# The attention products with the values stationary, in four column parts of the tensor engine

## The chip, the cores and the metric

The kernel runs on one core of one Trainium2 chip. The metric is the device time of one execution, in microseconds (us). A core has five engines that run side by side and meet through semaphores: TensorE (PE, matrix products into the PSUM banks), VectorE (DVE), ScalarE (ACT, activation functions), GpSimd (POOL) and SyncE (SP, which issues all DMAs of this kernel). Every engine works through its own instructions strictly in the order in which they were written.

## The reference, cut to what matters

Inputs are q, k and v of shape 8 x 8 x 576 x 64 (batch, head, position, channel) and the parameters of a feed-forward part.

```python
scores = q @ k.T / sqrt(64);  mask: block i sees blocks j <= i, blocks of 64
attn   = exp(scores - max);   attn = attn / sum(attn)
x      = concat over heads of attn @ v             # 8 x 576 x 512
x_prev = x shifted by one position inside a batch
xk = mu_k * x + (1 - mu_k) * x_prev                # the "mix"
xr = mu_r * x + (1 - mu_r) * x_prev
k  = relu(xk @ w_k);  v = (k * k) @ w_v            # 512 -> 1024 -> 512
out = sigmoid(xr @ w_r) * v
```

The kernel leaves out the subtraction of the maximum. It forms the sigmoid from a tanh, with the factor one half folded into `w_v`.

## The kernel before, in words

The positions of all batches, 8 x 576 = 4,608, form one row. Attention works by batch (`b`), the feed-forward part by chunks (`c`) of 512 positions, nine of them; a chunk crosses the border between two batches.

For each batch q and k are loaded, cast to bf16 and turned so that the channel lies on partitions (for the first two batches by PE products, `add_long_qkt`; for the others by a DMA transpose, `add_qk`). `add_scores` multiplies k by q, two heads side by side in the two halves of PE's rows (L675). ACT takes the exponential (L697), which gives unnormalized probabilities with key positions on partitions; POOL sets the masked corners to zero (L705). An `e` buffer holds the probabilities of one pair of heads; there are three.

`add_av` (L717) then takes each head's 128 x 128 pieces of the probabilities as the stationary operand and streams the values, 64 columns and a column of ones, past them: 15 products per head (L738). The result has the query position on partitions, the 65th column is the sum. DVE takes the reciprocal of the sums (L758, five per partition) and multiplies (L759) into the tile `x`. `add_xt` (L802) turns `x` on PE in fp32 (L812), four 128 x 128 pieces to one PSUM bank, and ACT copies the turned pieces into `xt` (L791), which has channels on partitions and positions along the row.

`add_mix` (L840) forms the difference to the previous position (`d`, L851, on POOL or DVE) and from it xk and xr (L863, DVE). `add_pk` multiplies by `w_k` (L899), ACT applies the relu (L909) and DVE squares (L915). `add_pr` multiplies by `w_r` (L928), ACT takes the tanh (L938). `add_pv` multiplies the squares by `w_v` (L957), DVE multiplies by tanh plus one (L967), and SP stores the result (L973).

The order of the instructions is fixed when the program is built. Every step is a task with an engine, an estimated duration, a rank, the tasks that it depends on and the buffers that it takes. `Plan.order` runs through time with these estimates: an engine that is free takes the task of lowest rank whose dependencies and buffers are ready by the estimates. `RANK` holds the ranks, the order of the loads, and for `flex` tasks the engine. The rings give the number of buffers: PSUM has two banks for scores (`s`, each two banks wide), two for attention results (`m`) and two for the feed-forward part (`mm`); batch 0's attention results use `mm`. On the chip an instruction that isn't ready holds everything behind it on its engine. `fill` tasks (L996) are products of an identity matrix with no use for the result; they come last in rank and so stand where the plan has nothing else for PE.

Of the kernel before, what the change touches and what calls it, by code (L numbers as in the profile page):

```python
# [24 lines left out]
RANK = {  # L25
 'loads': ['g0q', 'g0k', 'v4', 'b1g0q', 'g1q', 'v2', 'wk4', 'wv3', 'g1k',
           'wk6', 'b1g1k', 'v0', 'v3', 'v1', 'wk1', 'b1g0k', 'wk3', 'b1v0',
           'wk0', 'mu', 'wr1', 'b1g1q', 'wk5', 'b1v2', 'wk2', 'wv7', 'wv2',
           'wk7', 'wv6', 'wv0', 'b1v3', 'wv5', 'wv1', 'wv4', 'b1v1',
           'b1v4', 'wr0', 'wr3', 'wr2'],  # L30
 'cast k': 73.0,
 'cast r': -238.0,
 'cast v': 217.5,
 'qkt0': [1111.0, 118.5],
 'score0': [-518.5, -654.0, -419.5, -913.5, -522.5, -642.5, -671.0, -497.0,
            -421.0, -801.5, -464.0, -766.0, -967.5],
 'av0': [-570.0, -764.5, -682.5, -522.0, -807.5, -750.0, -447.5, -733.0],
 'xt0': [-283.0, -183.5, -390.5, -555.0, -237.5],
 'mix0': [-428.0, -99.5, 191.5, 92.0],
 'pk0': [-241.5, -17.5, -339.0, -413.0, -149.5, -278.5, -81.5, -167.0],  # L40
 'pr0': [60.5, 55.5, -497.5, -275.5],
 'pv0': [62.0, -164.0, -8.0, 48.0],
 'qk': [33.5, 38.0, 37.0, 41.0],
 'v': 46.0,
 'qkt': [418.0, -487.5],
 'turn': -17.0,
 'av': -416.0,
 'xt': 6.5,
 'mix': 646.5,
 'xr': 4.0,  # L50
 'moe': 63.0,
 'eng': {'v32': 'POOL',
         'wk7': 'ACT',
         'qk201': 'DVE',
         'long0010': 'DVE',
         'v71': 'POOL',
         'd61': 'POOL',
         'd42': 'POOL',
         'qk701': 'DVE',
         'v70': 'ACT',  # L60
         'd02': 'POOL',
         'd41': 'DVE',
         'v64': 'DVE',
         'qk511': 'DVE',
         'v72': 'DVE',
         'long0000': 'DVE',
         'wv0': 'POOL',
         'd33': 'POOL',
         'qk611': 'DVE',
         'qk300': 'POOL',  # L70
         'd51': 'POOL',
         'v23': 'POOL',
         'long0110': 'DVE',
         'qk501': 'POOL',
         'd10': 'POOL',
         'ev0010': 'DVE',
         'v03': 'POOL',
         'd01': 'POOL',
         'long1110': 'DVE',
         'qk700': 'ACT',  # L80
         'v20': 'POOL',
         'v01': 'DVE',
         'qk601': 'POOL',
         'qk321': 'POOL',
         'v14': 'POOL',
         'qk620': 'POOL',
         'v51': 'ACT',
         'd20': 'DVE',
         'v41': 'POOL',
         'qk331': 'POOL',  # L90
         'qk430': 'POOL',
         'd32': 'POOL',
         'qk520': 'POOL',
         'long0001': 'ACT',
         'd53': 'POOL',
         'd81': 'POOL',
         'v73': 'DVE',
         'v40': 'ACT',
         'd31': 'POOL',
         'qk221': 'ACT',  # L100
         'd43': 'DVE',
         'qk420': 'ACT',
         'qk211': 'POOL',
         'v43': 'POOL',
         'qk730': 'POOL',
         'v21': 'POOL',
         'v54': 'DVE',
         'qk720': 'POOL',
         'wk6': 'POOL',
         'qk320': 'POOL',  # L110
         'd72': 'POOL',
         'v62': 'POOL',
         'd62': 'POOL',
         'qk500': 'POOL',
         'qk401': 'POOL',
         'v31': 'DVE',
         'd52': 'POOL',
         'long1111': 'POOL',
         'wv6': 'POOL',
         'v63': 'POOL',  # L120
         'wk0': 'ACT',
         'qk411': 'DVE',
         'qk510': 'DVE',
         'long0011': 'ACT',
         'v50': 'ACT',
         'd22': 'POOL',
         'v00': 'ACT',
         'qk210': 'ACT',
         'v61': 'DVE',
         'd82': 'POOL',  # L130
         'ev0000': 'ACT',
         'qk630': 'POOL',
         'v53': 'POOL',
         'v60': 'POOL',
         'v10': 'POOL',
         'wr2': 'POOL',
         'd23': 'DVE',
         'qk721': 'POOL',
         'qk421': 'POOL',
         'd11': 'POOL',  # L140
         'long1000': 'DVE',
         'qk310': 'POOL',
         'qk710': 'POOL',
         'long0111': 'POOL',
         'ev0101': 'DVE',
         'qk311': 'ACT',
         'wk2': 'DVE',
         'd71': 'POOL',
         'v52': 'POOL',
         'qk530': 'ACT',  # L150
         'qk220': 'ACT',
         'v04': 'POOL',
         'd73': 'DVE',
         'qk610': 'DVE',
         'd80': 'POOL',
         'long1100': 'POOL',
         'd60': 'POOL',
         'qk631': 'POOL',
         'qk600': 'POOL',
         'd83': 'POOL',  # L160
         'qk400': 'ACT',
         'v74': 'POOL',
         'v44': 'DVE',
         'v42': 'DVE',
         'long0100': 'DVE',
         'qk531': 'ACT',
         'long0101': 'DVE',
         'd70': 'POOL',
         'd40': 'POOL',
         'qk301': 'POOL',  # L170
         'qk330': 'POOL',
         'd63': 'POOL',
         'qk231': 'POOL',
         'qk230': 'POOL',
         'v30': 'POOL',
         'd30': 'POOL',
         'qk711': 'DVE',
         'ev0001': 'ACT',
         'd50': 'DVE',
         'qk521': 'POOL',  # L180
         'long1101': 'DVE',
         'wk3': 'DVE',
         'qk431': 'POOL',
         'd00': 'POOL',
         'qk621': 'ACT',
         'qk731': 'ACT',
         'd03': 'POOL',
         'wk5': 'POOL',
         'qk410': 'DVE',
         'v02': 'POOL',  # L190
         'ev0011': 'DVE',
         'v34': 'POOL',
         'qk200': 'POOL',
         'long1001': 'POOL',
         'ev1011': 'ACT',
         'v22': 'POOL',
         'wv5': 'POOL',
         'wk4': 'POOL',
         'wv4': 'DVE',
         'v11': 'POOL',  # L200
         'wr1': 'POOL',
         'v13': 'ACT',
         'long1010': 'POOL',
         'long1011': 'POOL',
         'v33': 'POOL',
         'wk1': 'DVE',
         'wv1': 'ACT',
         'wv7': 'POOL',
         'd12': 'DVE',
         'ev1000': 'ACT',  # L210
         'wv2': 'DVE',
         'd13': 'POOL',
         'ev0111': 'ACT',
         'ev1010': 'ACT',
         'v12': 'POOL',
         'ev1101': 'DVE',
         'ev1111': 'ACT',
         'wv3': 'ACT',
         'd21': 'DVE',
         'ev0100': 'DVE',  # L220
         'ev1110': 'DVE',
         'wr0': 'ACT',
         'ev1001': 'ACT',
         'ev0110': 'DVE',
         'v24': 'ACT'},
}


class Plan:
# [4 lines left out]
    LATENCY = {"PE": 0.12, "ACT": 0.08, "DVE": 0.08, "POOL": 0.1, "SP": 2.4}  # L234
# [85 lines left out]
def kernel(  # L320
# [21 lines left out]
    D1 = D + 1  # L342
# [6 lines left out]
    RINGS = {"ld": 10, "vl": 5, "nl": 4, "nb": 4, "tl": 2, "qkt": 2, "e": 3,  # L349
             "x": 4, "r": 4, "xt": 2, "d": 3, "xk": 2, "xr": 2, "kr": 3,  # L350
# [17 lines left out]
    identf = consts.tile([P, P], FP)  # L368
    make_identity(nc, identf)
    VOs = [consts.tile([P, 5, H, D1 + 1], F16, name=f"VO{i}") for i in range(2)]  # L370
    E4s = [consts.tile([P, H, P], F16, name=f"EL{i}") for i in range(2)]
# [11 lines left out]
    for i in range(2):  # L383
        nc.vector.memset(VOs[i][:, :, :, D:D1], 1.0)
        nc.vector.memset(VOs[i][D:P, 4], 0.0)
        nc.vector.memset(E4s[i], 0.0)
    for nb in NBs:
        nc.gpsimd.memset(nb[D:P, :, 4], 0.0)
# [23 lines left out]
    def flex(key, alts, rank, fn, deps, takes=(), uses=()):  # L412


        eng = RANK["eng"].get(key, next(iter(alts)))
        t = plan.add(eng, alts[eng], rank, lambda: fn(eng), deps, takes, uses)
        t["key"], t["alts"] = key, alts
        return t
# [22 lines left out]
    def add_qk(b, pr, rank, turn_rank):  # L441
        nb = plan.buf("nb")
        for n, src in enumerate((q, k)):
# [10 lines left out]
            def fn(eng, n=n, key=key):  # L454
# [7 lines left out]
                f"qk{b}{pr}{n}", {"POOL": 0.76, "DVE": 0.7, "ACT": 0.65}, rank, fn,  # L462
# [46 lines left out]
    CAST = {"POOL": 0.72, "DVE": 0.77, "ACT": 0.7}  # L509
# [36 lines left out]
    def add_v(b, ranks):  # L546
        for sc in range(5):
# [8 lines left out]
            def fn(eng, n=n, sc=sc):  # L556
                convert(eng, VOs[b % 2][0:n, sc, :, 0:D],
                        tiles["vl", b, sc][0:n])
            cast["v", b, sc] = flex(
                f"v{b}{sc}", {"POOL": 0.73, "DVE": 0.7, "ACT": 0.65},  # L560
# [4 lines left out]
    def add_w(name, n, ranks, rank):  # L565
        src = {"k": moe_w_k, "r": moe_w_r, "v": moe_w_v}[name]
        src = src.rearrange("(cc p) (n j) -> n cc p j", p=P, j=C)
        for i in range(n):
            ld = plan.buf("ld")
            cc, half = (i % CCn, i // CCn) if name == "k" else (i, 0)  # L570
            t = load(("w", name, i), lambda: new("ld", [P, S], FP),
                     lambda d, cc=cc, half=half: [(d[:, 0:C], src[half, cc])],
                     ranks[i], 0.8, takes=[ld])


# [525 lines left out]
```

The softmax here doesn't subtract the row's maximum and nothing guards it: scores larger than these inputs give would overflow.

## Time and profile before

| What | Value |
|---|---|
| Three runs | 274.95, 276.27, 277.6 us (median 276.27) |
| Profiled execution, span | 274.9 us (the page gives no other time for it) |
| PE, products | 262.7 us busy, 96% (2,676 instructions) |
| PE, weight loads | 151.8 us, 55% |
| DVE | 209.1 us, 76% |
| ACT | 196.6 us, 72% |
| POOL | 129.3 us, 47% |
| DMA, share of the engines | 82% over the span; near one until about 210 us, low afterwards |
| Value products (L738) | 960, 193 ns each from start to end |
| Turning products (L812) | 160, 273 ns each from start to end |
| Copies into `xt` (L791) | 68, 23.1 us |
| Normalization (L758, L759) | 64 of each, 188 and 492 ns |

The span runs from the first instruction to the last. Products are pipelined: the duration of one, from its start to its end, is much longer than the distance to the next, so counts times durations say little for PE, and a busy PE is not one at its peak. For the other engines the distance is close to the duration. The granted PE clock was 0.998 of full speed.

### The profile page before, as it was taken

How to read it: one execution, taken by the hardware profiler on the slowest of the kernel's cores; microseconds unless marked ns; L12 is line 12 of the kernel's file. 1: busy time of each engine (PE TensorE's matmuls, PEld its weight loads, DVE VectorE, ACT ScalarE, POOL GpSimd, SP SyncE). 2: the span in 40 equal slices, each digit the busy share in tenths (PEclk: the TensorE clock that was granted, in tenths of full speed). 3: DMA queues.
4: the chain of work that ended last, by engine and by line, in shares of the span. 5: the costliest groups of instructions: out<-in, count | busy, mean ns of one | idle time of the engine just before them, and what ended most of it. 6: DMA issues, size and time to landing. Idle time of an engine off the chain costs nothing.

```text
span 274.9 us, 7043 instructions
## 1 busy us (share of the span) xinstructions
PE 262.7 (96%) x2676; PEld 151.8 (55%) x2676; DVE 209.1 (76%) x373; ACT 196.6 (72%) x315; POOL 129.3 (47%) x275
## 2 busy tenths in 40 slices
PE   8989997999999999999999999989999999999995
PEld 8777774555465546555654465446554655444443
DVE  4647796789789767897988687938898876996642
ACT  2689886876898688887888888776867883460630
POOL 3156898364457465573661353733845152601000
PEclk9999999999999999999999999999999999999999
DMA  7989999789999999999989988999999002102113
GB/s 221 346 237 263 308 325 213 170 191 203 239 189 214 214 207 245 206 207 214 232 169 235 206 222 196 220 205 259 193 195 257 4 0 79 76 0 88 66 41 114
DMA packets 137617, 51.32 MB, mean 187 GB/s; under 512 B 128240, under 2 KB 128496, under 8 KB 137584
## 3 DMA queue, kind: packets, MB, share of 16 engines
q1 hardware_dynamic: 137584, 50.88, 82.4%
q8 instruction: 21, 0.34, 0.5%
q14 instruction: 12, 0.10, 0.1%
HBM read 33.56 MB, written 9.44 MB: 156 GB/s over the span
## 4 chain that ended last, share of the span: by engine, by line
PE 65%; DMA 11%; DVE 9%; POOL 7%; issue 3%; SPq 3%; ACT 1%; POOLq 0%; DVEq 0%; ACTq 0%
PE t_mm L899 18%; PE t_mm L957 18%; PE t_mm L928 8%; PE t_m L738 8%; PE t_s L675 6%; PE t_m L812 4%; DMA t_ld<-in_k_dram 4%; SPq L406 2%; DVE t_xk L863 2%; DMA t_ld<-in_q_dram 2%; POOL WV L431 2%; DVE t_xr L863 2%; DMA t_vl<-in_v_dram 2%; DMA t_ld<-in_moe_w_k_dram 2%; DVE t_x L759 1%
## 5 line engine op out<-in xcount | busy, mean ns | idle before, releaser
L697 ACT ACTIVATE t_e<-t_s 128x1024 f16<-128x1024 f32 x96 | 96.3, 1027 | 15.8 <-PE t_s L675 15.5
L899 PE MATMUL t_mm<-t_xk,WK 128*128 128x512 f16 x288 | 68.9, 380 | 1.5 <-ACT t_kr L909 0.6
L957 PE MATMUL t_mm<-WV,t_k 128*128 128x512 f16 (+1 forms) x296 | 67.0, 373 | 0.0
L915 DVE TENSOR_TENSOR t_k<-t_kr 128x512 f16<-128x512 f32 x72 | 55.0, 775 | 13.5 <-ACT t_kr L909 13.2
L909 ACT ACTIVATE t_kr<-t_mm 128x512 f32<-128x512 f32 x72 | 42.9, 598 | 15.8 <-PE t_mm L899 13.7
L705 POOL MEMSET t_e<- 64x128 f16 x128 | 24.8, 210 | 56.3 <-ACT t_e L697 50.4
L957 PEld LDWEIGHTS <-t_k 128*128 128x128 f16 x296 | 28.1, 98 | 31.4 <-issue 2.0
L899 PEld LDWEIGHTS <-WK 128*128 128x128 f16 x288 | 25.5, 97 | 31.6 <-issue 6.3
L851 POOL TENSOR_TENSOR t_d<-t_xt 128x512 f32<-128x512 f32 x28 | 32.7, 1175 | 17.2 <-DVE t_xr L863 6.9
L738 PEld LDWEIGHTS <-t_e 128*128 128x128 f16 x896 | 33.0, 97 | 13.4 <-issue 3.2
L938 ACT ACTIVATE t_t<-t_mm 128x512 f32<-128x512 f32 x36 | 21.7, 603 | 22.4 <-PE t_mm L928 20.7
L967 DVE SCALAR_TENSOR_TENSOR t_o<-t_t,t_mm 128x512 f32<-128x512 f32 (+1 forms) x37 | 24.7, 669 | 14.9 <-PE t_mm L957 11.4
L928 PE MATMUL t_mm<-WR,t_xr 128*128 128x512 f16 x144 | 36.0, 379 | 0.0
L863 DVE SCALAR_TENSOR_TENSOR t_xk<-t_d,MUK,t_xt 128x512 f16<-128x512 f32 x36 | 33.4, 929 | 2.5 <-POOL t_d L851 2.3
L675 PE MATMUL t_s<-t_qkt 64*128 64x64 bf16 (+4 forms) x384 | 32.0, 277 | 2.6 <-DVE t_qkt L429 0.8
L738 PE MATMUL t_m<-VO,t_e 128*128 128x65 f16 x784 | 31.1, 193 | 2.6 <-POOL VO L429 2.5
L863 DVE SCALAR_TENSOR_TENSOR t_xr<-t_d,MUR,t_xt 128x512 f16<-128x512 f32 x36 | 31.8, 894 | 0.0
L759 DVE TENSOR_TENSOR t_x<-t_m,t_r 128x320 f32<-128x320 f32 x56 | 27.5, 492 | 1.9
L791 ACT COPY t_xt<-t_m 128x256 f32<-128x256 f32 (+7 forms) x68 | 23.1, 407 | 7.0 <-PE t_m L812 6.8
L675 PEld LDWEIGHTS <-t_qkt 64*128 64x128 bf16 x384 | 12.8, 94 | 19.8 <-issue 10.8
L429 POOL CAST NB<-t_ld 128x512 bf16<-128x512 f32 x28 | 19.5, 701 | 7.9 <-DMA t_ld<-in_q_dram 6.7
L812 PE MATMUL t_m<-identf,t_x 128*128 128x128 f32 x160 | 22.7, 276 | 0.3 <-DVE t_x L759 0.3
(54 smaller groups left out, 235.8 us busy)
## 6 DMA issues: line engine op xcount, KB each, us to landing
out_dram<-t_o SPq DMA_DIRECT2D x35, 256.0 KB, 3.0
t_vl<-in_v_dram SPq DMA_DIRECT2D x32, 256.0 KB, 4.5
t_ld<-in_q_dram SPq DMA_DIRECT2D x48, 128.0 KB, 3.9
t_ld<-in_k_dram SPq DMA_DIRECT2D x48, 128.0 KB, 3.5
t_ld<-in_q_dram SPq DMA_DIRECT2D x8, 288.0 KB, 4.8
t_ld<-in_k_dram SPq DMA_DIRECT2D x8, 288.0 KB, 6.3
t_ld<-in_moe_w_k_dram SPq DMA_DIRECT2D x8, 256.0 KB, 6.5
t_ld<-in_moe_w_v_dram SPq DMA_DIRECT2D x8, 256.0 KB, 6.6
```

What stands on the lines that cost most here:

```text
L675: nc.tensor.matmul(PS[:, h, col:col + n], qkt[rows, pr, 1, kc * P:kc * P + P], qkt[rows, pr, 0, q0:q0 + n], start=True, stop=True)
L697: nc.scalar.activation(tiles["e", b, pr][:, :, i, :], tiles["ps", b, it], AF.Exp, scale=ISQ)
L738: nc.tensor.matmul(PA[:, mt * D1:(mt + 1) * D1], stationary(b, h, kc, mt), VOs[b % 2][:, kc, head, 0:D1], start=(kc == 0), stop=(kc == mt))
L759: nc.vector.tensor_tensor(tiles["x", b, blk][:, :, head % 2 * D:(head % 2 + 1) * D], view[:, :, 0:D], Rc[:, :].unsqueeze(2).to_broadcast([ ...
L812: nc.tensor.matmul(px[:, i * P:(i + 1) * P], src, identf, is_transpose=True, start=(i == 0), stop=(i == 3))
L851: (nc.vector if eng == "DVE" else nc.gpsimd).tensor_tensor(tiles["d", c, cc], x[:, cc, 1:CH + 1], x[:, cc, 0:CH], ALU.subtract)
L863: nc.vector.scalar_tensor_tensor(tiles[name, c][:, cc], tiles["d", c, cc], (MUK1, MUR1)[n][:, cc:cc + 1], tiles["xt", c][:, cc, 1:CH + 1], ...
L899: nc.tensor.matmul(ps, WK[:, cc, jc * P:(jc + 1) * P], tiles["xk", c][:, cc], start=(cc == 0), stop=(cc == CCn - 1))
L909: nc.scalar.activation(tiles["kr", c, jc], tiles["pk", c, jc], AF.Relu)
L915: nc.vector.tensor_tensor(tiles["k2", c][:, jc], KR, KR, ALU.mult)
L928: nc.tensor.matmul(ps, tiles["xr", c][:, cc, jt * P:(jt + 1) * P], WR[:, cc], start=(cc == 0), stop=(cc == CCn - 1))
L957: nc.tensor.matmul(ps[:, 0:w], tiles["k2", c][:, jc, jt * P:(jt + 1) * P], WV[:, jc, cols], start=(jc == 0), stop=(jc == JCn - 1))
```

## The change

The roles of the two operands of the value product are exchanged. The values are stationary, the probabilities stream past them. Four heads, a half batch `Q`, go together: each takes 32 of PE's 128 columns (`tile_position`), so one group of four products fills all 128 partitions of the result with 32 of the 64 channels of each head, and a second group takes the other 32. The result has channels on partitions and positions along the row, which is the layout of `xt`. The sums come from the same streams past `THIRD`, a stationary operand whose columns are ones in every third place; the three thirds of the 576 positions land in different rows of one bank. DVE takes the reciprocal of 192 per partition, spreads each third to all 32 rows of its head with `stream_shuffle`, and multiplies the products straight into `xt`. The tile `x`, the turning products, their copies and the column of ones are gone.

Because the channels now lie in another order, the rows of `w_k` and `w_r` and the elements of `mu` are loaded in that order. Each half batch is two PE tasks: the sums and the first part of the positions, then the other two parts. Probabilities have four `e` buffers. The squares may go to DVE, ACT or POOL. The plan's estimated durations, its ranks, the engines of the `flex` tasks and the order of the loads are new.

```diff
-    D1 = D + 1
+    G = 4
+    W3 = S // 3
...
-    RINGS = {"ld": 10, "vl": 5, "nl": 4, "nb": 4, "tl": 2, "qkt": 2, "e": 3,
-             "x": 4, "r": 4, "xt": 2, "d": 3, "xk": 2, "xr": 2, "kr": 3,
+    RINGS = {"ld": 10, "vl": 5, "nl": 4, "nb": 4, "tl": 2, "qkt": 2, "e": 4,
+             "c": 2, "rd": 2, "xt": 2, "d": 3, "xk": 2, "xr": 2, "kr": 3,
              "k2": 1, "t": 3, "o": 3, "s": 2, "m": 2, "mm": 2, "vo": 2, "el": 2}
...
-    VOs = [consts.tile([P, 5, H, D1 + 1], F16, name=f"VO{i}") for i in range(2)]
-    E4s = [consts.tile([P, H, P], F16, name=f"EL{i}") for i in range(2)]
+    VOs = [consts.tile([P, 5, H, D], F16, name=f"VO{i}") for i in range(2)]
+    E4s = [consts.tile([P, H, D], F16, name=f"EL{i}") for i in range(2)]
+    THIRD = consts.tile([P, 34], F16)
...
+    nc.vector.memset(THIRD, 0.0)
+    nc.vector.memset(THIRD[:, 0:34:3], 1.0)
...
+            src = src.rearrange("(q g s r) (n j) -> n q s g r j", g=G, s=2,
+                                r=D // 2, j=C)
...
+    def add_values(b, Q, ranks):
...
+        def products(ps, lhs, a, z, last):
+            for kc in range((z + P - 1) // P):
+                q0 = max(a, kc * P)
+                for g in range(G):
                     nc.tensor.matmul(
+                        ps[g * R:g * R + R, q0 - a:z - a], lhs(kc, g),
+                        probs(b, 4 * Q + g, kc, q0, z - q0),
+                        start=(kc == 0 and last is not None),
+                        stop=(kc == (z - 1) // P and last is not False),
+                        tile_position=(0, g * R))
+
+        def sums():
+            PS = tiles["den", b, Q] = new(ring, [P, CH], FP)
...
+            for t in range(3):
+                a, z = t * W3, t * W3 + W3
+                for kc in range((z + P - 1) // P):
+                    q0 = max(a, kc * P)
+                    for g in range(G):
+                        nc.tensor.matmul(
+                            PS[g * R:g * R + R, q0 - a:W3],
+                            THIRD[:, (3 - t) % 3:(3 - t) % 3 + R],
+                            probs(b, 4 * Q + g, kc, q0, z - q0),
...
+                            tile_position=(0, g * R))
+
+        def part(i):
+            a, z = parts[i]
+            PS = tiles["num", b, Q, i] = new(ring, [P, CH], FP)
+            w = z - a
+            for x in range(2):
+                products(PS[:, x * w:x * w + w],
+                         lambda kc, g: VOs[b % 2][:, kc, 4 * Q + g,
+                                                  x * R:x * R + R],
+                         a, z, True)
...
+        for v, mine in enumerate(([0], [1, 2])):
+            bufs = [plan.buf(ring) for _ in mine]
+            dbuf = plan.buf(ring) if v == 0 else None
...
+            t = on("PE", 0.1 + (0.68 if v == 0 else 0)
+                   + sum(cost(i) for i in mine), ranks[v], fn, deps + vdeps,
+                   takes=([dbuf] if v == 0 else []) + bufs,
+                   uses=ebufs + [vo_buf[b], el_buf[b]])
...
+                    nc.vector.reciprocal(tiles["c", b, Q],
+                                         tiles["den", b, Q][:, 0:W3])
...
+                        nc.vector.stream_shuffle(
+                            tiles["rd", b, Q][:, t * W3:t * W3 + W3],
+                            tiles["c", b, Q], [t] * 32)
...
+                    nc.vector.tensor_tensor(
+                        xt_tile(c)[:, 2 * Q:2 * Q + 2, 1 + at:1 + at + w],
+                        tiles["num", b, Q, i][:, 0:2 * w].rearrange(
+                            "p (s t) -> p s t", s=2),
+                        tiles["rd", b, Q][:, a:z].unsqueeze(1).to_broadcast(
+                            [P, 2, w]), ALU.mult)
...
-    def to_xt(key, b, t0, n, off, cc, deps, rank, uses):
...
-    def add_xt(b, pr, rank):
...
+        def sq(eng):
+            KR, K2 = tiles["kr", c, jc], tiles["k2", c][:, jc]
+            if eng == "ACT":
+                nc.scalar.activation(K2, KR, AF.Square)
+            else:
+                (nc.vector if eng == "DVE" else nc.gpsimd).tensor_tensor(
+                    K2, KR, KR, ALU.mult)
...
-        nc.sync.dma_start(MUK, moe_mu_k.rearrange("(cc p) -> p cc", p=P))
-        nc.sync.dma_start(MUR, moe_mu_r.rearrange("(cc p) -> p cc", p=P))
+        for dst, src in ((MUK, moe_mu_k), (MUR, moe_mu_r)):
+            src = src.rearrange("(q g s r o) -> q s g r o", g=G, s=2, r=D // 2,
+                                o=1)
+            for cc in range(CCn):
+                nc.sync.dma_start(
+                    dst[:, cc:cc + 1], src[cc // 2, cc % 2])
...
-        for h in range(H):
-            add_av(b, h, r + (R["av"] + 3 * (h // 2) + h % 2 if b else
-                              R["av0"][h]))
-        for pr in range(HP):
-            add_xt(b, pr, r + (R["xt"] + 3 * pr if b else R["xt0"][pr]))
-        add_xt(b, HP, r + (R["xt"] + 3 * HP if b else R["xt0"][HP]))
+        for Q in range(2):
+            add_values(b, Q, [r + (R["av"][2 * Q + v] + R["avb"][b] if b else
+                                   R["av0"][2 * Q + v]) for v in range(2)])
```

In the changed program the value products stand in line 609, the sums in line 624.

## The prediction, made before the changed kernel was run

> **What bounds the kernel now.** I began with the page: busy shares, then the forty slices.
>
> ```profile
> span 274.9 us, 7043 instructions
> ...
> PE   8989997999999999999999999989999999999995
> ...
> DVE  4647796789789767897988687938898876996642
> ACT  2689886876898688887888888776867883460630
> ```
>
> TensorE (PE) is full from the seventh slice to the last; VectorE (DVE) and ScalarE (ACT) stand at seven to nine tenths. Filler products make the early PE digits high, so I asked for stretches cut at the first feed-forward product (41 us).
>
> ```profile
> 41.00:100.00 59.00, 56.07 (x537) 30.94 (x537) 47.30 (x85) 45.55 (x77) 32.99 (x72) 1.00 1.04 205
> 100.00:160.00 60.00, 59.54 (x605) 32.91 (x605) 49.06 (x92) 50.35 (x82) 30.99 (x69) 1.00 1.12 217
> 160.00:210.00 50.00, 48.63 (x463) 26.22 (x457) 41.01 (x73) 37.94 (x63) 28.26 (x60) 1.00 0.97 208
> 210.00:235.00 25.00, 25.00 (x250) 14.10 (x243) 19.19 (x38) 17.37 (x30) 6.86 (x17) 1.00 0.18 64
> ```
>
> Columns: stretch, length, busy time of PE, weight loads, DVE, ACT, GpSimd (POOL), then clock, DMA share, GB/s. PE idles 4.8 of 194 us: what leaves PE shortens this stretch, until another engine binds. DVE is at 156.6/194 = 81%. From 235 us only feed-forward products are left. The chain of waits prices the parts by where the next one starts:
>
> ```profile
> 129.69 0.91 PE t_m L738 x30
> 130.60 0.86 PE t_mm L899 x4
> ...
> 134.75 0.87 PE t_m L812 x8
> 135.62 0.54 PE t_s L675 x6
> 136.16 0.97 PE t_mm L899 x4
> ```
>
> A value product costs 0.91/30 = 30.3 ns, a turning product (L812) 0.87/8 = 109 ns, a 512-column product 0.86/4 = 215 ns, so a column 0.42 ns. After scores (L675, two half-height parts of PE) the next four cost 0.97: leaving the parts costs 0.11. Do parts run together? The PE timeline shows it for half height:
>
> ```profile
> 124.98 0.51 PE L675 MATMUL t_s<-t_qkt 64*128 64x320 bf16 x12
> 125.42 2.76 PE L899 MATMUL t_mm<-t_xk,WK 128*128 128x512 f16 x12
> ```
>
> These twelve are 2 of 320, 2 of 192 and 8 of 64 columns, 1,536 in all. In turn they take 0.65 us; two at once 0.32, and 0.11 to leave: 0.43, and the next starts after 0.44. Four column parts appear nowhere.
>
> DVE's prices (groups, each shape apart):
>
> ```profile
> L915 DVE TENSOR_TENSOR t_k<-t_kr 128x512 f16<-128x512 f32 x72 | 55.0, 775 | 13.5 <-ACT t_kr L909 13.2
> L759 DVE TENSOR_TENSOR t_x<-t_m,t_r 128x320 f32<-128x320 f32 x56 | 27.5, 492 | 1.9
> L758 DVE RECIPROCAL t_r<-t_m 128x5 f32<-128x5 f32 x56 | 10.5, 188 | 7.9 <-PE t_m L738 7.9
> L851 DVE TENSOR_TENSOR t_d<-t_xt 128x512 f32<-128x512 f32 x8 | 6.7, 836 | 0.7 <-ACT t_xt L791 0.7
> ```
>
> [...] L863 shows a 746 ns median and a maximum of 1,992[...].
>
> **The change, part by part.**
>
> *PE.* Gone: 960 x 30.3 ns = 29.1 us and 160 x 109 ns = 17.4 us, 46.5 together. Per head the causal products stream 576+448+320+192+64 = 1,600 columns, once per value half: 2 x 1,600 x 64 heads = 204,800; the row sums (`THIRD`) stream them once more, 102,400. At 0.42 ns and four at a time: 307,200/4 x 0.42 = 32.3 us. The 1,904 products form 476 groups of four, 161 columns (68 ns) a group on average. Bounds of this unknown: 32 us if loads hide;[...] 129 us if nothing overlaps. I take 32, since the half-height parts hide theirs. Each of 32 blocks leaves the mode: 32 x 0.11 = 3.5. Net 35.8 - 46.5 = -10.7 us; an eighth is the first batch's, before 41 us under loading, so **-9.4** on the path.
>
> *ACT.* 68 copies (23.1 us) go; 11 squares at about 0.6 and eleven more casts and copies (about 6) come: some 10 us less. Not the bound; counted nothing, and with that cover gone it would be PE's waits on exponentials again.
>
> *DVE.* Gone: 64 x (188+492) ns = 43.5 us. Added: 16 reciprocals over 192, never seen. [...] 48 normalizations, 18,432 elements[...]. Sum 65.3, or +21.8 net. 35 squares leave (-27.1), 12 differences come (+10.0), casts net about +5. DVE grows by some 10 us, roughly 9 of them in the stretch: 165 in about 184, 90%.
>
> *POOL.* 12 differences fewer (-14), 24 squares more at the difference's 1,175 ns (+28), fewer casts (-18): about -4. Two WV casts of 1.6 us less stand in line there; the chain of waits runs over three of them (39.6 to 45.4 us). I credit **-1.5** (0 to -3).
>
> *A new wait.* `m` keeps two PSUM banks. The first block of a half batch fills both (sums, part 0); its second needs both back, after reciprocal 1.34, three shuffles 1.07 and the 256-wide normalization 0.69: 3.1 us, with some 0.3 for handovers. In the new PE order 2.6 to 5 us of other products lie between, mostly about 3. Behind the waiting block stand scores and feed-forward in order. 14 blocks x 0 to 1 us; I take 0.2: **+3**.
>
> *Loads.* The same bytes. `mu` becomes eight descriptor sets instead of two: six more on SP's queue near 25 us, before WR; at some 0.55 us an issue up to 3 us of issuing, hidden while DMA is full there, otherwise +1. Rows of WK and WR stay 2 KB pieces. More of batch 1's attention now stands ahead of the first feed-forward product; this moves work and adds none. The last load is issued at 208 us while batch 7's last scores run at 226: 18 us of slack before loading could cap a gain. The `e` ring of four replaces three, since a block holds two pairs: nothing (to +2 if exponentials wait). After the last score the PE order holds about the same 44 us as before: no change at the end.
>
> Sum: -9.4 - 1.5 + 3 = -7.9. The profiled execution's span is 274.9, within the runs (274.95 to 277.6, median 276.27) but for the time around it, at most 1.4 us against the median; I apply the sum to that: 268.4.
>
> **Rivals.**
>
> *The loads take turns.* [...] The place is every group of L609/L624; it decides from 91 ns a group upward, where PE's saving is gone. [...] Against it: paired half-height loads hide behind 64 columns.
>
> *DVE binds.* At 90% it would exceed its densest whole stretch (81-82%). If it sustains only about 86%, 165/0.86 = 192 us against 194: -2, so 274.3. For it: squares and reciprocals share one in-order queue.[...]
>
> *The bank wait is long.* 14 blocks at 1 us: 279.
>
> *The parts don't overlap* (the change doesn't do what it says): 129+3.5-46.5 = +86, of it 75 on the path, 352.
>
> **How the numbers follow.** Forecast 0.66 (its own range 258 to 273), DVE binds 0.12, bank wait 0.05, loads in turn 0.14, no overlap 0.03. Faster by over 1%: 0.66; within 1% (about what this measurement can tell from no change): 0.12; slower: 0.05+0.14+0.03 = 0.22. The range 258 to 282 covers the first three, 0.83.
>
> **What would show it.** PE's groups: four column products starting a few ns apart, 0.67 us for the forty sums and 68 ns a group of values[...]. DVE: reciprocals near 1.34, shuffles near 0.36, its share in the middle near 90%. Idle PE ended by a normalization ahead of second blocks beyond 0.2 us each means the bank wait. I am wrong if PE falls idle behind DVE or if groups are paced by loads.

## The result, and the profile after

The changed kernel takes 308.9 us (307.6 to 310.0) where the kernel before takes 276.9 on the same chip: a ratio of 1.118, with a 95% interval of 1.112 to 1.125. The forecast was 268.4, faster. The profiled execution has a span of 308.1 us, 33.2 more than before.

The page of the changed kernel, the lines that answer to those shown of before, with the PE clock and the DMA engines:

```profile
span 308.1 us, 8562 instructions
...
PE   8399832414979999879999999998999999997995
...
DVE  1244513756399757868899996789499969997432
ACT  1058940344774898568759977974885795261440
...
PEclk9789995955899999979999999999999999999999
DMA  5999527544998899999989999998989901201103
```

The DMA engines of the kernel before, in slices of 6.9 us:

```profile
DMA  7989999789999999999989988999999002102113
```

A slice of the changed kernel is 7.7 us. From the eleventh slice on PE is nearly as full as it was before. The loss is ahead of that: from 38 to 77 us PE stands at one to four tenths, its clock falls to a half in three of these five slices, and the DMA engines, which were seven to nine tenths busy in this stretch before, stand at two to seven. The stretches of the same kernel (columns as in the prediction):

```profile
40.00:60.00 20.00, 6.50 (x218) 4.59 (x207) 7.79 (x18) 5.25 (x7) 8.03 (x12) 0.74 0.53 125
60.00:80.00 20.00, 7.97 (x74) 3.57 (x73) 10.10 (x19) 8.11 (x13) 4.26 (x10) 0.57 0.49 136
80.00:140.00 60.00, 55.18 (x725) 26.35 (x728) 45.07 (x83) 44.59 (x66) 25.73 (x60) 0.97 1.02 213
140.00:200.00 60.00, 59.52 (x806) 28.54 (x794) 52.85 (x102) 48.70 (x72) 30.49 (x66) 1.00 1.02 211
```

From 40 to 80 us no engine is busy for half of the time, PE for 14.5 of the 40 us, and the DMA engines are half idle too, at 125 and 136 GB/s against 213 and 211 from 80 to 200 us. Everything waits. The first feed-forward product starts at 75.4 us; before it was 40.1. The lines of the PE timelines that begin with it, before and after:

```profile
40.08 0.61 PE L899 MATMUL t_mm<-t_xk,WK 128*128 128x512 f16 x2
75.41 4.69 PE L821 MATMUL t_mm<-WR,t_xr 128*128 128x512 f16 x12 [0.38 <-ACT WR L280]
```

From there to the last product it is 229.5 us, before 231.7: the long stretch that should have become 9 us shorter became 2 us shorter.

The column parts themselves do what was forecast. The PE timeline of the changed kernel:

```profile
150.96 0.85 PE L624 MATMUL t_m<-t_e,THIRD 128*32 128x192 f16 x36
151.63 0.20 PE L624 MATMUL t_m<-EL,THIRD 128*32 128x64 f16 x4
151.66 0.29 PE L609 MATMUL t_m<-t_e,VO 128*32 128x128 f16 x8
151.88 0.61 PE L539 MATMUL t_s<-t_qkt 64*128 64x512 bf16 x6
```

The forty sums take 0.70 us from the first start to the first value product (0.67 forecast). Inside, the four products of a group start 2 to 4 ns apart, and one group of 192 columns follows the next after 83 ns in the median, close to the streaming time of 192 x 0.42 = 81 ns. The four weight loads of a group start 3 to 4 ns apart as well, and they hide. Each lasts 92 to 98 ns from start to end in these sums.

DVE's new groups:

```profile
L670 DVE RECIPROCAL t_c<-t_m 128x192 f32<-128x192 f32 x14 | 18.9, 1351 | 6.2 <-PE t_m L624 6.1
L678 DVE STREAM_SHUFFLE t_rd<-t_c 128x192 f32<-128x192 f32 x48 | 14.7, 369 | 0.0
L690 DVE TENSOR_TENSOR t_xt<-t_m,t_rd 128x384 f32<-128x384 f32 x20 | 10.9, 550 | 1.7 <-PE t_m L609 1.6
```

A reciprocal takes 1,351 ns for 1,340 forecast, a shuffle 369 for some 360. No trace of before shows either: the two forecasts did not rest on one. A normalization of 384 elements takes 550 ns, one of 512 (256 positions) 681. By counts times durations the 16 reciprocals, 48 shuffles and 48 normalizations make 65.7 us, for 65.3 forecast.

To see where the 33 us are, each product on PE is given the time from its start to the start of the next, at most to its own end; the rest is idle. Worked out from the trace, in us:

| PE's time | Before | After | Even/odd (below) |
|---|---|---|---|
| Value and turning products; then column products | 51.2 | 39.4 | 39.0 |
| Feed-forward products | 159.3 | 166.5 | 166.5 |
| Scores | 27.9 | 30.9 | 30.4 |
| Filler, turning q and k | 24.3 | 26.8 | 26.1 |
| Idle | 7.7 | 39.9 | 15.7 |
| Sum | 270.4 | 303.5 | 277.8 |

The saving is there, 11.8 us. Idle time takes 32.2 back, and the other products 12.7.

Why everything waits in the start is told by the queue that issues the loads. SP's waits on loads of `w_k` in the first 20 us (in total, times, longest, in us), before and in the changed kernel, where they are its costliest:

```profile
SPq L406 <- DMA t_ld<-in_moe_w_k_dram: 0.3, 1, 0.3
SPq L263 <- DMA t_ld<-in_moe_w_k_dram: 6.4, 2, 4.6
```

The load order of the changed kernel begins with two loads of WK, issued at 0.7 and 1.5 us. In the trace SP's ninth and tenth load wait for the semaphores that these two raise on landing, and go out at 7.1 and 12.0 us; behind them stand the rest of q, and k. In the trace's record of packets, a mean of 4.1 packets of 2 KB is in flight from 4 to 10 us, at most 6; in the kernel before, with plain rows, it is 12.3 (30 to 36 us). 4.2 are in flight again from 65 to 75 us, with the DMA engines otherwise little used (a share of 0.39 in all). A packet of 2 KB takes 84 ns in the median over either run, so the packets aren't slower; fewer go side by side. The changed load takes its rows in four groups of 32, the load of before 128 in one run. Why so few packets of the four groups are in flight is not shown: the trace doesn't say which engine carried a packet.

From 38 to 77 us the loads of the weights hold up DVE and ACT, which also work in order. From the list of waits of the changed kernel, those that belong to the two longest stops of PE (in total, times, longest, in us):

```profile
PE t_mm L624 <- DVE t_xt L690: 10.7, 1, 10.7
DVE WR L286 <- DMA t_ld<-in_moe_w_r_dram: 5.6, 1, 5.6
PE t_s L539 <- ACT t_e L561: 10.0, 5, 7.4
ACT WR L280 <- DMA t_ld<-in_moe_w_r_dram: 8.7, 3, 6.2
```

In the first (41.0 to 51.7 us) PE waits for banks that DVE's normalization has to free. On DVE this stands behind a cast of `w_r` that waits 5.6 us for its load, and before it 2.9 and 2.3 us went in waiting for the two `mu`. In the second (58.9 to 66.3 us) PE waits for an exponential, which stands on ACT behind a cast of `w_r` that waits 6.2 us. With natural rows (first experiment below) PE waits at most 4.0 us in one piece ahead of the first feed-forward product, and 1.4 us for these banks.

### The profile page after: what moved, and what is told of

Same layout as the page of the kernel before. It is cut to its first block, busy times and chain, and to the rows that moved or that the text cites. A ratio compares the mean times of both kernels' runs of the same rounds, so it can differ in the third digit from the quotient of the medians.

```text
span 308.1 us, 8562 instructions
## 1 busy us (share of the span) xinstructions
PE 263.6 (86%) x3460; PEld 139.6 (45%) x3460; DVE 213.4 (69%) x395; ACT 186.6 (61%) x268; POOL 125.3 (41%) x262
## 5 line engine op out<-in xcount | busy, mean ns | idle before, releaser
L539 PE MATMUL t_s<-t_qkt 64*128 64x64 bf16 (+4 forms) x384 | 34.4, 285 | 12.4 <-ACT t_e L561 10.0
L850 PEld LDWEIGHTS <-t_k 128*128 128x128 f16 x296 | 27.9, 98 | 34.6 <-issue 3.6
L807 DVE TENSOR_TENSOR t_k<-t_kr 128x512 f16<-128x512 f32 x37 | 28.8, 789 | 19.2 <-ACT t_kr L798 19.0
L821 PE MATMUL t_mm<-WR,t_xr 128*128 128x512 f16 x144 | 38.1, 395 | 1.6 <-DVE t_o L860 1.2
L807 POOL TENSOR_TENSOR t_k<-t_kr 128x512 f16<-128x512 f32 x24 | 27.9, 1172 | 23.1 <-ACT t_kr L798 22.6
L752 DVE SCALAR_TENSOR_TENSOR t_xk<-t_d,MUK,t_xt 128x512 f16<-128x512 f32 x36 | 33.2, 937 | 5.0 <-POOL t_d L740 4.4
L860 DVE SCALAR_TENSOR_TENSOR t_o<-t_t,t_mm 128x512 f32<-128x512 f32 (+1 forms) x37 | 24.7, 667 | 12.3 <-PE t_mm L850 8.5
L740 POOL TENSOR_TENSOR t_d<-t_xt 128x512 f32<-128x512 f32 x16 | 20.5, 1284 | 20.6 <-DVE t_xt L690 12.0
L539 PEld LDWEIGHTS <-t_qkt 64*128 64x128 bf16 x384 | 13.0, 95 | 34.8 <-issue 27.9
L609 PEld LDWEIGHTS <-VO 128*32 128x32 f16 x1264 | 23.2, 98 | 5.6 <-issue 5.1
L893 PE MATMUL t_mm<-identb 128*128 128x128 bf16 x300 | 22.9, 236 | 2.2 <-POOL identb masks.py:199 1.4
L609 PE MATMUL t_m<-t_e,VO 128*32 128x192 f16 (+3 forms) x976 | 24.3, 242 | 0.0
L690 DVE TENSOR_TENSOR t_xt<-t_m,t_rd 128x384 f32<-128x384 f32 (+3 forms) x42 | 22.3, 549 | 2.0 <-PE t_m L609 1.6
L670 DVE RECIPROCAL t_c<-t_m 128x192 f32<-128x192 f32 x14 | 18.9, 1351 | 6.2 <-PE t_m L624 6.1
```

Of the source, the lines that this page charges most:

```text
L539: nc.tensor.matmul(PS[:, h, col:col + n], qkt[rows, pr, 1, kc * P:kc * P + P], qkt[rows, pr, 0, q0:q0 + n], start=True, stop=True)
L609: nc.tensor.matmul(ps[g * R:g * R + R, q0 - a:z - a], lhs(kc, g), probs(b, 4 * Q + g, kc, q0, z - q0), start=(kc == 0 and last is not None ...
L752: nc.vector.scalar_tensor_tensor(tiles[name, c][:, cc], tiles["d", c, cc], (MUK1, MUR1)[n][:, cc:cc + 1], tiles["xt", c][:, cc, 1:CH + 1], ...
L807: (nc.vector if eng == "DVE" else nc.gpsimd).tensor_tensor(K2, KR, KR, ALU.mult)
L821: nc.tensor.matmul(ps, tiles["xr", c][:, cc, jt * P:(jt + 1) * P], WR[:, cc], start=(cc == 0), stop=(cc == CCn - 1))
L850: nc.tensor.matmul(ps[:, 0:w], tiles["k2", c][:, jc, jt * P:(jt + 1) * P], WV[:, jc, cols], start=(jc == 0), stop=(jc == JCn - 1))
```

## The experiments

### Which rows are loaded

**Natural rows of `w_k` and `w_r` in the changed kernel.** The rows then don't belong to the operand's channels; the amount of work is the same.

```diff
-            src = src.rearrange("(q g s r) (n j) -> n q s g r j", g=G, s=2,
-                                r=D // 2, j=C)
+            src = src.rearrange("(cc p) (n j) -> n cc p j", p=P, j=C)
```

> The changed kernel, with w_k and w_r loaded in their plain row order as before (so the feed-forward part multiplies by rows in another order than the channels have, and the output differs); the instructions and their order are those of the changed kernel otherwise. Theory A (the permuted row loads [...]hold everything behind them, 12 loads): the first feed-forward product moves from about 72 us to 42-50 us, the time falls by 25 us or more, to 268-284. Rival B (the new order of the loads is what starts late: weights and batch 1 ahead of k): still late, 300 or more. Rival C (batch 0's long chain through two PSUM banks): still late, 300 or more.

Measured: 285.4 us, ratio 1.034 (1.026 to 1.041); the first feed-forward product at 50.0 us. The form of twelve loads is worth 23.5 of the 32 us. It is 1 us above the upper end that theory A allowed: 8 to 10 us have another cause.

**The row order alone, in the kernel before.** Here, too, the rows then belong to other channels than the operand's.

```diff
-        src = src.rearrange("(cc p) (n j) -> n cc p j", p=P, j=C)
+            src = src.rearrange("(q g s r) (n j) -> n q s g r j", g=4, s=2,
+                                r=D // 2, j=C)
```

> The kernel before, with only the row order of the w_k and w_r loads changed to the permuted one (so the output differs). Theory A: the start gets later by 10 us or more and the time rises to 287-310. Rivals B and C: no change, 274-280.

Measured: 297.6 us against 275.6, ratio 1.079 (1.071 to 1.086). Without a single column product, the same loads cost 22 us; 3.4 packets of 2 KB are in flight from 30 to 36 us, at most 6. The chain of work that ended last now has, by line (whole line of the page):

```profile
PE t_mm L963 21%; PE t_mm L905 19%; PE t_mm L934 10%; DMA t_ld<-in_moe_w_k_dram 9%; PE t_m L744 8%; PE t_s L681 7%; PE t_m L818 5%; DMA t_ld<-in_k_dram 4%; DMA t_ld<-in_moe_w_r_dram 3%; SPq L406 2%; DMA t_qkt<-NB 2%; PE t_mm L1002 2%; ACT t_e L703 1%; DVE t_xk L869 1%; DVE t_k L921 0%
```

9% and 3% of the span are loads of these weights, on the path itself.

**Each permuted load cut into four of 32 rows.**

```diff
-                          (d[:, 0:C], src[half, cc] if name == "v" else
-                           src[half, cc // 2, cc % 2])],
+                          (d[:, 0:C], src[half, cc])] if name == "v" else [
+                          (d[g * 32:g * 32 + 32, 0:C],
+                           src[half, cc // 2, cc % 2, g]) for g in range(G)],
```

> The changed kernel, each permuted w_k or w_r load issued as four plain loads of 32 rows, 48 issues instead of 12, everything else the same. Theory A: if a 32-row load spreads over the DMA engines, 270-290, the extra issues costing a few us of SP's queue against e1; if each again stays on few engines, 300 or more. Rivals B and C: 305-315.

Measured: 297.5 us, ratio 1.077 (1.068 to 1.085), which neither theory named. More packets go side by side, a mean of 7.2 from 2 to 5 us, where such loads are nearly alone. But 12 loads have become 48. In the first 5 us of the kernel before, an issue of q or k takes SP 0.43 us in the median; by an estimate from this the 36 more keep it busy some 15 us longer. It recovers a third of the loss; that the issues cost the rest was not tested apart.

**Even and odd channels.** If the two groups of a head take its even and its odd channels, row 2p + s of a block of 256 belongs to partition p: one even distance, 128 rows in one run. `mu` needs one load each again.

```diff
-            src = src.rearrange("(q g s r) (n j) -> n q s g r j", g=G, s=2,
-                                r=D // 2, j=C)
+            src = src.rearrange("(q p s) (n j) -> n q s p j", p=P, s=2, j=C)
...
-                         lambda kc, g: VOs[b % 2][:, kc, 4 * Q + g,
-                                                  x * R:x * R + R],
+                         lambda kc, g: VOs[b % 2][:, kc, 4 * Q + g, x:D:2],
...
-            src = src.rearrange("(q g s r o) -> q s g r o", g=G, s=2, r=D // 2,
-                                o=1)
-            for cc in range(CCn):
-                nc.sync.dma_start(
-                    dst[:, cc:cc + 1], src[cc // 2, cc % 2])
+            nc.sync.dma_start(dst.rearrange("p (q s) -> p q s", s=2),
+                              src.rearrange("(q p s) -> p q s", p=P, s=2))
```

> The changed kernel in full, with another split of the 64 channels: the two groups of a head take its even and its odd channels instead of its lower and upper half. The rows that a weight load needs then lie at one even distance (row 2p + s of a block of 256), so one load is a single run of 128 rows again, and mu needs one load each. Theory A [...]: [...]first scores near 13 us or earlier, first feed-forward product at 44 to 49 us, time 278 to 287. Rival (any row order but the natural one is slow, or mu and the weight columns at a distance of two cost as much): [...]the groups of four column products take more than 82 ns for 192 columns; time above 292.

Measured: 283.8 us, ratio 1.025 (1.020 to 1.031). 10.8 packets of 2 KB are in flight from 2 to 4 us, at most 17, and SP's waits on these loads in the first 20 us shrink from 6.4 to this:

```profile
SPq L263 <- DMA t_ld<-in_moe_w_k_dram: 1.0, 1, 1.0
```

The groups of 192 columns still follow each other after 83 ns, so weight columns at a distance of two cost nothing that shows here. The first scores come at 18.9 us instead of 24.9 (not at 13, as expected), the first feed-forward product at 49.1. This version does all that the changed kernel does, and 25.1 of its 32.0 us are gone: the pattern of the rows, and with it the number of packets that go side by side, was the cause of these. The packets in flight went with the pattern in the changed kernel and in the one before, under the same order of loads each time. That the permuted loads hold the rest up, as theory A has it, is shown; why their pattern leaves so few packets side by side is not. Against the natural rows (1.034), where `mu` still has eight loads, the difference of 1.6 us is within the intervals: no cost of these eight loads is shown. What remains to be explained are 6.9 us, and the 9.4 that were forecast as a gain.

### The order of the loads

**The load order of before in the changed kernel**, and the same in the even/odd version. Both edits put the kernel's old list in place:

```diff
- 'loads': ['wk2', 'wk7', 'g0q', 'b1g1q', 'b1g0q', 'g1q', 'g0k', 'b1v0',
+ 'loads': ['g0q', 'g0k', 'v4', 'b1g0q', 'g1q', 'v2', 'wk4', 'wv3', 'g1k',
...
```

> The changed kernel with the list of the loads' order taken from the kernel before (q and k of batch 0 first); the permuted loads stay, and the plan reorders around it. Theory A: the first scores come near 12 us, but the weights still arrive late and the first feed-forward product stays near 65 us or later: 298-312. Rival B: most of the loss is gone, 270-285.

> The even/odd version with the loads in the order of the kernel before. Theory A (what is left of the late start comes from two weight loads standing ahead of the first q and k): first scores near 10.5 us, first feed-forward product at 40 to 43 us, time 5 to 8 us below the even/odd version. Rival (the plan's ranks fit its own order of loads, and the other order only moves waits): the same or slower than the even/odd version by up to 12 us.

Measured: 323.3 us, ratio 1.171 (1.164 to 1.179), and 298.2 us, ratio 1.078 (1.071 to 1.085). Both are 14 us slower than the version they start from, though the first scores do come at 10.9 and 10.7 us. The second lies beyond even the 12 us that its rival allowed. So q ahead of the two weight loads doesn't win back what is left. But the plan places every instruction anew when the list changes, and these runs don't test the list alone: with the old list the even/odd version has 28.0 us of idle PE instead of 15.7, among it 5.6 us in one piece at 250 us, far from any of these loads.

### Is PE the bound after the start?

**Every sum twice.**

```diff
-            for t in range(3):
+            for t in (0, 1, 2, 0, 1, 2):
```

> The even/odd version with every row sum formed twice in place (same result): 102,400 columns more in four column parts, 10.7 us at 0.42 ns a column, 9.4 us of it after the first batch. Theory P (PE binds once the start is over): 8 to 12 us above the even/odd version. Rival W (waits set the pace in between, PE has slack): at most 4 us above it.

Measured: 291.0 us, 7.2 above the even/odd version, for 10.7 us of products (an estimate at 0.42 ns a column, as is the 20.6 below). That is just under what theory P (PE binds) asked for, and well over what rival W (waits set the pace) allowed.

**Only the first 128 keys in the column products.**

```diff
-            for kc in range((z + P - 1) // P):
+            for kc in range(1):
...
-                for kc in range((z + P - 1) // P):
+                for kc in range(1):
```

> The even/odd version with the column products of the first 128 keys alone; the sums and values of the keys from 128 on are left out, so the output is that of a shorter attention. 196,608 columns fewer, 20.6 us at 0.42 ns and four at a time, 18 us of it after the first batch; scores, exponentials and everything else stay. Theory P (PE binds): 14 to 20 us below the even/odd version. Rival W (exponentials, banks or the mode changes set the pace): at most 7 us below it.

Measured: 278.9 us, 5.0 below, for 20.6 us of products taken away. Rival W, clearly. The two results fit together if PE is nearly full as it is: work added lengthens the run, work taken away leaves holes. PE's idle time rises from 15.7 to 29.4 us. The mean granted clock falls too, from 0.976 to 0.963, and the feed-forward products take 2.3 us more. PE's longest waits from 50 to 280 us in this kernel:

```profile
PE t_mm L848 <- DVE t_o L858: 4.2, 5, 1.6
PE t_mm L786 <- POOL t_xk L765: 4.1, 4, 1.4
PE t_s L538 <- ACT t_e L560: 2.4, 3, 1.0
PE t_mm L786 <- ACT t_kr L796: 2.0, 4, 0.7
```

The feed-forward products now wait for their operands (`xk`, last touched on POOL after DVE's mix) and for DVE and ACT to empty their banks.

**VectorE lighter: a multiplication instead of the reciprocal**, in the even/odd version and together with the first keys only.

```diff
-                    nc.vector.reciprocal(tiles["c", b, Q],
-                                         tiles["den", b, Q][:, 0:W3])
+                    nc.vector.tensor_scalar_mul(
+                        tiles["c", b, Q], tiles["den", b, Q][:, 0:W3], 1e-5)
```

> The even/odd version with the 16 reciprocals of 192 per partition (1.35 us each, 21.6 us of VectorE) replaced by a multiplication with a constant, some 0.35 us each; the quotient is left out, so the outputs are not normalized. 16 us less on VectorE, nothing else changes. Theory D (VectorE is the second bound beside PE: its share is 83 to 88% in the middle, and most of what ends PE's waits once column products are left out is VectorE's): 2 to 6 us below the even/odd version. Rival (the waits come from the order, not from VectorE's load): within 1.5 us of it.

> Both at once: column products of the first 128 keys only (20.6 us less of PE) and the reciprocals replaced by a multiplication (16 us less of VectorE); sums and values of later keys and the quotient are left out. Theory D: the two bounds hide each other, so together they give clearly more than the 5 us of the shorter products and what the cheap reciprocal gives alone added up: 268 us or less. Rival (order): the sum of the two and no more, 275 to 278.

Measured: 279.9 us, 4.0 below the even/odd version, and 273.5, 10.3 below. These two ran on another chip than the even/odd version; by the ratios to the kernel before on each chip it is 3.3 and 9.8. Taking some 16 us from DVE (an estimate: 1.35 us less some 0.35 for each of 16, where a shuffle of the same size took 0.37) pays about a quarter, as taking 20 us from PE does, and together they pay 1.3 us more than the sum. So DVE is part of what holds PE, and theory D's first half stands, though the intervals of the two ratios only just miss each other. 273.5 lies between the ranges of both sides, nearer to the sum: DVE isn't a second bound that hides behind the first, for then both at once would have given far more. PE's waits for DVE, ACT and POOL in turn remain.

### Order, and the clock

**Placed anew.** The changed kernel's plan reckons 195 us of work for DVE, the trace of the even/odd version shows 214.

```diff
-    for t in plan.order():
-        t["fn"]()
+    for i in ORDER:
+        plan.tasks[i]["fn"]()
```

> The even/odd version in full with another order: the task list is placed anew with the durations that the trace of the even/odd version shows (the changed kernel's plan reckons 195 us of work for VectorE and 109 for GpSimd, the trace shows 214 and 123), some 140 casts, squares and differences change engine, and the order of every engine is given as a list. The work is the same. Theory O (what is left of the loss is the order, fitted to durations that are too short, so that PE waits): 266 to 276 us. Rival (PE and VectorE are full and no order helps): 280 us or more.

Measured: 298.8 us, ratio 1.082 (1.076 to 1.089), 15 us slower than the even/odd version; PE's idle time is 26.4 us. Theory O failed, and a better order was not found. The engines of 143 tasks changed with the order, and POOL is busy for 143.7 us instead of 123.0, so this run doesn't show the order alone. That a placement of the same work can cost about 15 us is shown twice (here and by the list of loads); that estimates which are too short are what is wrong with the plan is not shown.

**Filler where PE waits.** In the even/odd version PE waits 2.8 us at 37 us for a cast of batch 1's k, and 3.0 us in three pieces from 103 to 107 us. Products without use go into two places, that one and ahead of the last of these three pieces, into a bank that the next product overwrites.

```diff
+                    if (b, g, y, n) == (1, 1, 0, 1):
+                        for x in range(44):
+                            nc.tensor.matmul(tiles["pq", b, g, y, n][:, 0:P],
+                                             identb, identb, start=True,
+                                             stop=True)
...
+            if (c, jc) == (2, 0):
+                for x in range(26):
+                    nc.tensor.matmul(ps[:, 0:P], identb, identb, start=True,
+                                     stop=True)
```

> The even/odd version with 70 products of the identity matrix put in at two places where its trace shows PE waiting with nothing to do: 44 ahead of the turning product of batch 1's second half (2.8 us of waiting at 37 us) and 26 ahead of the first feed-forward product of the third chunk (1.6 us of waiting at 105 us). They write a bank that the next product overwrites; the useful work and its order are the same. Theory C (a stretch of waiting lowers the granted PE clock, and the products after it then run slower: 0.5 from 106 to 112 us, 0.67 to 0.81 from 38 to 50 us): the clock stays at 1.0 after 105 us, four products of 512 columns take 0.87 us there instead of 1.7, and the time falls by 2 to 5 us although work is added. Rival (the low clock has another cause, or what waits behind isn't PE-bound): within 1.5 us of the even/odd version, or above it.

The PE timeline of the even/odd version, and then of this one:

```profile
106.85 1.87 PE L786 MATMUL t_mm<-t_xk,WK 128*128 128x512 f16 x4 [1.62 <-POOL t_xk L765]
108.65 1.04 PE L538 MATMUL t_s<-t_qkt 64*128 64x320 bf16 x6
109.62 2.72 PE L786 MATMUL t_mm<-t_xk,WK 128*128 128x512 f16 x6
```

```profile
104.11 1.63 PE L792 MATMUL t_mm<-identb 128*128 128x128 bf16 x26
105.71 1.02 PE L795 MATMUL t_mm<-t_xk,WK 128*128 128x512 f16 x4
106.67 0.61 PE L543 MATMUL t_s<-t_qkt 64*128 64x320 bf16 x6
107.21 2.76 PE L795 MATMUL t_mm<-t_xk,WK 128*128 128x512 f16 x12
```

After the wait four products of 512 columns and the six scores behind them hold PE for 2.8 us (106.85 to 109.62), after the filler for 1.5 (105.71 to 107.21). The granted clock from 106 to 112 us was 0.50; with filler it is 1.00, in this execution over the whole span, which is 278.2 us instead of 282.3. The feed-forward products take 163.7 us of PE's time, 2.9 less.

Over all executions the gain is smaller: 282.8 us, ratio 1.019 (1.015 to 1.024), 1.0 below the even/odd version (1.7 by the ratios, since the chips differ) and with intervals that overlap. The clock's mean goes with it: it was 1.00 in one execution only (280.0 us) and 0.98 to 0.99 in the others (282.0 to 284.4), and 0.97 to 0.98 in all of the even/odd version (283.0 to 285.1). That the clock stays up when the wait is filled is shown in the profile; the gain in the median lies where the rival put it, below the 2 to 5 us of theory C. The trace of the even/odd version has the clock at 0.50 from 105.35 to 112.18 us: it fell when PE had waited 1.5 of the 3.0 us, as the longest of the three pieces began. This waiting lay within 2.2 us, with scores in between. With filler 1.4 us of waiting was left in this place, in two pieces.

## Why the prediction was wrong

| Step | Forecast, us | Measured, us |
|---|---|---|
| Column products for value and turning products, with leaving the parts | -10.7 on the span | -11.8 of PE's time (-12.2 even/odd); what entering a mode costs counts with the products ahead of it |
| ACT busy | -10 | -10.0 (196.6 to 186.6) |
| DVE busy | +10, 90% in the middle | +4.3 (209.1 to 213.4); 88% from 100 to 160 us, even/odd |
| POOL busy; credit on the path | -4; -1.5 | -4.0 (129.3 to 125.3); not seen |
| Wait for the two banks | +3 | no such wait in the list of PE's waits after 80 us |
| `mu` in eight loads | at most +1 | none shown (1.6 between natural rows and even/odd, within the intervals) |
| Rows of `w_k` and `w_r` | 0 | +25.1 together with `mu` (+22 in the kernel before, without) |
| The stretch after the first feed-forward product | -9.4 | -2.2 (231.7 to 229.5); -1.7 even/odd (230.0) |

**The step that failed first is "Loads".** It reads "The same bytes" and "Rows of WK and WR stay 2 KB pieces", and counts nothing. Bytes and piece size are right and don't matter: the pattern of the rows left these loads four packets in flight instead of 11 to 12, and what works in order waited on them, SP with q and k behind, DVE and ACT with normalizations and exponentials behind. This term, put at 0, measured 25.1 us. The prediction had put a price on every new operation and none on an old one with a new pattern. No rival covered it: "the loads take turns" meant PE's weight loads, and these hide (83 ns a group of 192 columns, for 81 of streaming).

**The second is the exchange of PE's time for the run's time.** "What leaves PE shortens this stretch, until another engine binds" took one for one. The PE term itself was right. Once the loads are mended, the sum would have given 268; it is 283.8. In the profiles the first feed-forward product of the even/odd version comes 9.1 us later than before (49.1 against 40.1), and the stretch after it is 1.7 us shorter, not 9.4. The table of PE's time shows how the even/odd version stands to before: -12.2 for the products, +8.0 idle, +7.2 on feed-forward products, +2.5 on scores, +1.9 on filler and turning, in all +7.4, which is the difference of the spans (282.3 to 274.9). Of the idle time, pieces over 0.25 us hold 6.6 us ahead of the first feed-forward product (before 1.7) and 7.4 after it (before 5.4). Of the +7.2, 2.9 went with the low clock in the profile with filler. Part of the remainder is in changes of PE's mode. Beyond the streaming of the product ahead, each costs 91 to 98 ns in the median, entering as much as leaving, and with 127 changes in place of 91 those without a wait sum to 11.7 us after the first feed-forward product, 2.9 more than before. The prediction had priced 3.5 for leaving 32 blocks and nothing for entering; that this sum came out nearly right is partly luck.

DVE binding, as the rival put it, is only partly so: DVE's share rose to 88% (53.1 of the 60 us from 100 on, even/odd), and lightening it pays about a quarter. That the fixed order makes PE wait for each engine in turn is argued, not shown. Why only a quarter is paid, and whether another order would pay it all, stays open: the two other placements that ran were slower by 14 and 15 us.

The phrase on the end, "no change", was off too: from the last score to the last product it was 45.6 us before and 49.4 after, in the even/odd version as well. This may be work that was moved there; no run tested it. Two readings at the start of the prediction were a little off, without bearing on the result: PE is full from the eighth slice, not the seventh, and the first feed-forward product starts at 40.1 us, not 41.

## What to carry to other kernels

When a change alters the layout of a result, follow the layout back to every load that must match it, and look at the pattern of its rows: as four groups of 32 a load kept 4.1 packets of 2 KB in flight here, as one run of 128 it kept 10.8 to 12.3. A split that keeps one even distance (even and odd instead of lower and upper half) was as fast as natural rows, within the intervals (ratios of 1.025 and 1.034). Time taken from an engine that is 96% busy is not time taken from the run when two others stand at 72 and 76% in a fixed order: here a microsecond taken from PE or from DVE paid about a quarter (5.0 us for some 20.6, 4.0 for some 16), and one added to PE cost two thirds (7.2 for some 10.7). A wait on PE was dearer than its length where the clock fell with it: in the two profiles four feed-forward products and six scores took 2.8 us in place of 1.5.

## What had not been expected of the hardware

- Loads of 128 rows of 2 KB kept 4.1 packets in flight as 4 groups of 32 rows, and 10.8 to 12.3 as one run.
- Four column parts of 32 columns stream 192 columns each in 83 ns together, all four weight loads hidden, with weight columns side by side or at a distance of two.
- A change of PE's mode (full, half rows, column parts) costs 91 to 98 ns in the median, entering as well as leaving.
- The granted clock fell to 0.50 for 6.8 us when PE had waited 1.5 us within 2.2, in three pieces with scores in between.
- A reciprocal of 192 elements per partition takes 1,351 ns, 3.7 times a shuffle of the same size (369).
